# Strided attention and two expert layers on one core: both batches' attention ahead of most of the first layer, and one exponential per slot with its sum

## The chip, the cores and the metric

The kernel runs on one core of one Trainium2 chip. The metric is the time of one execution in microseconds on the device. TensorE (PE in the profile) does matmuls, VectorE (DVE) and ScalarE (ACT) work on tiles in PSUM and SBUF, SyncE (SP) issues DMAs.

## The reference

Attention with 2 batches, 8 heads, 576 positions and head size 64. Heads 0 to 3 see the 32 last positions, heads 4 to 7 see the positions with the same remainder by 32:

```
scores = q @ k.T / sqrt(64)
mask   = (0 <= i - j < 32)               for heads 0 to 3
         (i >= j and i % 32 == j % 32)   for heads 4 to 7
attn   = exp(scores - rowmax), divided by (its row sum + 1e-9)
x      = (attn @ v), as 1152 tokens x 512
h      = ((x @ w1) * (x @ w2)) @ w3 @ w_out          # moe_w1 ... moe_w_out
p      = probs / (row sum + 1e-9)
out    = sum over 4 experts of p[:, e] * (relu(h @ e_w1[e]) @ e_w2[e])
```

The inputs w1, w2, w3 and w_out arrive as 64-bit floats, all others as 32-bit floats.

## The kernel before

**Precision.** A product of two fp32 matrices is done in three matmuls (mm3, lines 245 to 249): each operand is split into a high part (a ScalarE copy that rounds) and a low part (a VectorE subtract), and high x high, low x high and high x low are added up in PSUM.

**Weights.** A 64-bit weight chunk of 128 x 1024 is loaded as pairs of integers and turned to fp32 by a row of steps: round_up (ACT, L136), magnitude (ACT, L144; for the first chunk DVE, L142), clamp, shift, sign, add (DVE, L147 to L157), split_hi (ACT, L164) and split_lo (DVE, L174). There are 20 such chunks: 8 of w12 (both w1 and w2 for 128 columns), 4 of w_out, 8 of w3. A generator, work(), emits their steps in this order, four stops a chunk; advance(n) lets it go n stops on. It is called between other work, so its instructions are woven into the engines' queues, which run in order. add() also issues the load of the chunk two places on (load_next); the raw tiles have two buffers. The variable live counts how many of the 16 buffers for split weights and attention values are in use; while it is over 14, work() doesn't split another chunk. A w12 chunk is freed when its last unit (batch 1, second half) has been emitted.

**Attention.** Each batch has six chunks (Chunk4): three of the local heads (g = 0, six slots of 64 keys per partition) and three of the strided heads (g = 1, eight slots of 54 keys). A chunk goes through scores (PE: a mask matmul and 32 or 48 small ones into one bank of ps_sc), maxima (DVE: row maxima per slot, then scores minus maxima into an SBUF frame), exps (ACT: one Exp over all slots), sums (DVE: sum per slot, + 1e-9, reciprocal), normalise (DVE), transposes (PE) and evac (ACT), pv (PE, two banks), put (ACT, x_hi) and put_lo (DVE, x_lo). The function attend(b, s) is one step of a pipeline of four chunks: scores, maxima and exps of chunk s, sums and normalise of chunk s - 1, transposes and evac of s - 2, pv, put and put_lo of s - 3. Nine steps finish a batch.

**First layer.** A unit (ab_block) is one batch, one of eight column blocks ft and one half of the batch's tokens: 12 matmuls of 288 columns with w1, 12 with w2, a copy (ACT, L444), a product (DVE, L446) and the split of the product (L448, L450). run_unit emits one, with two calls of advance in it. There are 32 units; all of a batch's x is read by each.

**Order of emission.** The queues' order is written out by hand (tc.manual_schedule):

```
for s in range(9):            # batch 0's attention
    attend(0, s)
    keep_warm(12)             # 12 filler matmuls that nobody reads
    if s > 3:
        advance(2)
load_qk(1, 1); load_v_str(1)
while done < 16:              # batch 0's 16 units, batch 1's attention between them
    run_unit()
    if done in (2, 4, 5, 7, 8, 10, 11, 13, 14):
        attend(1, next(steps))
load_probs()
while done < 32:              # batch 1's 16 units
    run_unit()
```

Behind it stand the product of w3 and w_out (wc_tile, eight tiles, wc_acc), the layer x3 with it, and the four experts in 32 steps. PSUM banks: five (pool ps) in turn for transposes, pv results, unit results and filler, three (ps_sc) for scores.

Of the kernel before, what the change touches and what calls it, by code (L numbers as in the profile page):

```python
# [8 lines left out]
F32 = mybir.dt.float32  # L9
# [4 lines left out]
AF = mybir.ActivationFunctionType  # L14
ALU = mybir.AluOpType

B, H, S, D = 2, 8, 576, 64
NT, DM, DFF, E = 1152, 512, 1024, 4
P = 128
# [13 lines left out]
SCALE = 1.0 / float(D) ** 0.5  # L33
# [9 lines left out]
def kernel(  # L43
# [13 lines left out]
    nc = tc.nc  # L57
# [8 lines left out]
    small = ctx.enter_context(tc.tile_pool(name="small", bufs=4))  # L66
# [125 lines left out]
    def load_next():  # L192
        nonlocal loaded
        if loaded < len(stream):
            stream[loaded].raw_load()
            loaded += 1
# [40 lines left out]
    def advance(n=1):  # L237

        return all([next(worker, False) for _ in range(n)])

    def need(c, part=0):
        while not (c.done if part == 0 else c.done1 if part == 1 else c.done2):
            assert advance()
# [12 lines left out]
    def load_qk(b, g, cut=0):  # L256

        tq, tk = (big[b].tile([P, 2, S], F32, tag="big", name=name) for name in ("tq", "tk"))
        pairs = slice(2 * g, 2 * g + 2)
        for c in ([slice(0, cut), slice(cut, S)] if cut else [slice(0, S)]):  # L260
            for t, src, queue in ((tk, kT, nc.sync), (tq, qT, nc.scalar if cut else nc.sync)):
                queue.dma_start(out=t[:, :, c], in_=src[b, pairs, :, c].rearrange("k p n -> p k n"))
        qk[b, g] = (tq, tk)

    def load_v_loc(b, c):

        tv = wp.tile([P, 2, 3, P], F32, tag="w", name="tv_loc")

        def load(dst, rows, t0, n):
            nc.sync.dma_start(out=dst, in_=v_loc[b, :, rows, t0:t0 + n].rearrange("k p t d -> p k t d"))  # L270

        lower, upper, middle = slice(0, 64), slice(64, P), slice(W, 3 * W)
        if c == 0:
            load(tv[lower, :, 0:1], lower, 0, 1)
            load(tv[upper, :, 0:1], middle, 0, 1)
            load(tv[:, :, 1:], slice(0, P), 1, 2)
        elif c == 1:
            load(tv, slice(0, P), 3, 3)
        else:
            load(tv[lower, :, 0:1], lower, 0, 1)  # L280
            load(tv[upper], middle, 3, 3)
            load(tv[lower, :, 1:], middle, 1, 2)
        vals[b, 0, c] = tv

    def load_v_str(b):

        threes = [wp.tile([P, n, P], F32, tag="w", name="tv_str") for n in (8, 4)]
        for tv, t0, n in ((threes[0], 0, 4), (threes[1], 4, 1)):
            for k in range(2):
                nc.sync.dma_start(out=tv[64 * k:64 * k + T3, :2 * n].rearrange("p (h t) d -> p h t d", h=2),  # L290
                                in_=v_str[b, k, :2 * T3, t0:t0 + n].rearrange("(h p) t d -> p h t d", h=2))
        for k in range(2):
            nc.sync.dma_start(out=threes[1][64 * k:64 * k + NB, 2:], in_=v_str[b, k, 2 * T3:2 * T3 + NB, :2])
        vals[b, 1] = threes

    class Chunk4:
# [44 lines left out]

        def maxima(self):
            s = self.slots
            mx = small.tile([P, 8], F32, tag="mx", name="mx")
            nc.vector.tensor_reduce(out=mx[:, :s], in_=self.sc, axis=mybir.AxisListType.X, op=ALU.max)
            self.frame = p_ring[self.index % 4]
            self.p = self.frame[:, :s, :self.nk]
            nc.vector.tensor_tensor(out=self.p, in0=self.sc, in1=self.wide(mx), op=ALU.subtract)

        def wide(self, t):  # L350
            return t[:, :self.slots].unsqueeze(2).to_broadcast([P, self.slots, self.nk])

        def exps(self):
            nc.scalar.activation(self.p, self.p, AF.Exp, scale=SCALE)

        def sums(self):
            s = self.slots
            self.rec = small.tile([P, 8], F32, tag="rec", name="rec")
            rec = self.rec[:, :s]
            nc.vector.tensor_reduce(out=rec, in_=self.p, axis=mybir.AxisListType.X, op=ALU.add)  # L360
            nc.vector.tensor_scalar_add(rec, rec, 1e-9)
            nc.vector.reciprocal(rec, rec)

# [68 lines left out]
    def ab_block(b, ft, n):  # L432
        t = slice(b * S + n * HB, b * S + n * HB + HB)
        if n == 0 and ft % 2 == 0:
            ab_hi[b, ft // 2] = big[b].tile([P, 2, S], F32R, tag="big", name="ab_hi")
            ab_lo[b, ft // 2] = big[b].tile([P, 2, S], F32R, tag="big", name="ab_lo")
        hi, lo = (x[b, ft // 2][:, ft % 2, n * HB:n * HB + HB] for x in (ab_hi, ab_lo))
        ab = tmp.tile([P, HB], F32, tag="pT", name="ab")
        for w in range(2):
            acc = bank("ab_acc")[:, :HB]  # L440
            for k in range(4):
                mm3(acc, c_w12[ft].parts((w * 4 + k) * P, P), (x_hi[:, k, t], x_lo[:, k, t]), k == 0, k == 3)
            if w == 0:
                nc.scalar.copy(ab, acc)  # L444
            else:
                nc.vector.tensor_tensor(out=ab, in0=acc, in1=ab, op=ALU.mult)  # L446
            yield
        nc.scalar.copy(hi, ab)  # L448
        yield
        nc.vector.tensor_tensor(out=lo, in0=ab, in1=hi.bitcast(F32), op=ALU.subtract)  # L450
        yield
# [68 lines left out]
    class Weights:  # L520
# [17 lines left out]
        def work(self):  # L538
# [20 lines left out]
            if self.again:  # L559
                for i, u in enumerate(sums):  # L560
                    nc.sync.dma_start(out=u.bitcast(F32), in_=stored[self.at][i])
            else:
                yield from self.split(sums, w)
                for i, u in enumerate(sums):
                    nc.sync.dma_start(out=stored[self.at][i], in_=u.bitcast(F32))
# [110 lines left out]
    def load_probs():  # L676
        den = const.tile([P, NTT], F32, name="den")
        nc.sync.dma_start(out=pn, in_=probs)
        nc.vector.tensor_reduce(out=den, in_=pn, axis=mybir.AxisListType.X, op=ALU.add)
        nc.vector.tensor_scalar_add(den, den, 1e-9)  # L680
        nc.vector.reciprocal(den, den)
        nc.vector.tensor_tensor(out=pn, in0=pn, in1=den.unsqueeze(2).to_broadcast([P, NTT, E]), op=ALU.mult)
# [4 lines left out]
    with tc.manual_schedule():  # L687
# [3 lines left out]
        p_ring = []  # L691
# [5 lines left out]
        strided_masks()  # L697
        load_v_loc(0, 0)
        load_qk(0, 1)
        load_next()  # L700
        load_v_loc(0, 1)
        load_v_loc(0, 2)
        load_v_str(0)
        load_next()
        load_qk(1, 0)
        for c in range(3):
            load_v_loc(1, c)
        chunks = [[Chunk4(3 * g + c, b, g, c) for g in range(2) for c in range(3)] for b in range(B)]
        units = [(b, ft, i) for b in range(B) for ft in range(8) for i in range(2)]
        done = 0  # L710

        rest = iter(())
# [1 line left out]
        def run_unit():  # L714

            nonlocal done, rest
            b, ft, i = units[done]
            need(c_w12[ft])
            block = ab_block(b, ft, i)
            for _ in range(2):  # L720
                next(rest, None)
                next(block)
                advance(1)
            rest = block
            done += 1
            if b == i == 1:
                c_w12[ft].free()

        def attend(b, s):

            nonlocal live
            chunk = chunks[b]
            n = len(chunk)
            if s < n:
                chunk[s].scores()
                chunk[s].maxima()
                chunk[s].exps()
            if 1 <= s <= n:
                chunk[s - 1].sums()
                chunk[s - 1].normalise()  # L740
            if 2 <= s < n + 2:
                chunk[s - 2].transposes()
                chunk[s - 2].evac(nc.scalar.copy)
            if 3 <= s:
                c = chunk[s - 3]
                c.pv()
                c.put()
                c.put_lo()
                if c.g == 0 or c.c > 0:
                    live -= 1  # L750

        for s in range(9):
            attend(0, s)
            keep_warm(12)
            if s > 3:
                advance(2)
        load_qk(1, 1)
        load_v_str(1)
        steps = iter(range(9))
        while done < 16:  # L760
            run_unit()
            if done in (2, 4, 5, 7, 8, 10, 11, 13, 14):
                attend(1, next(steps))
        load_probs()
        while done < 32:
            run_unit()
        for _ in rest:
            pass
# [4 lines left out]
        for it in range(8):  # L773
# [8 lines left out]
            i = {1: 0, 3: 1, 6: 2}.get(it)  # L782
# [32 lines left out]
        for c in wc[:3]:  # L815
# [6 lines left out]
        steps = [Step(half, e, c, c_e[16 * i + 4 * e + c])  # L822
                 for i, half in enumerate(halves) for e in range(E) for c in range(4)]
# [100 lines left out]
```

## Time and profile before

| | us |
|---|---|
| median of 2 runs | 645.09 (644.95 to 645.22) |
| profiled execution | 647.48 |
| its span, first to last instruction | 645.70 |
| PE busy in the span | 625.6 |
| VectorE busy | 455.9 |
| ScalarE busy | 265.2 |
| mean granted clock of TensorE | 0.992 |

All times in rows are microseconds from the start of the span, durations of single instructions in nanoseconds where a column says mean ns. An idle time in brackets is that of the engine in front of the row, with the instruction that ended it. The matmuls are pipelined, so that a matmul's duration is longer than the distance to the next one's start.

### The profile page before, as it was taken

The page shows a single profiled execution, that of the slowest core. Times are in us where ns is not written, and L with a number is a line of the kernel's source. Part 1 is how long each engine was busy: PE and PEld are TensorE (multiplying, and loading weights), DVE is VectorE, ACT ScalarE, POOL GpSimd, SP SyncE. Part 2 cuts the span into 40 slices and gives each one's busy share as a digit, 9 for nine tenths or more (in the row PEclk, how much of TensorE's full clock was granted, in tenths as well). Part 3 has the DMA queues.
Part 4 walks back from the last instruction along what each step waited for, and adds up shares of the span by engine and source line. Part 5 has one row for each costly group of instructions (what it writes and reads, how often), then busy time and mean ns, then how long its engine had stood idle before and what let it go on. Part 6 is the DMA issues. An engine that isn't in the chain of part 4 may idle for free.

```text
span 645.7 us, 11487 instructions
## 1 busy us (share of the span) xinstructions
PE 625.6 (97%) x4712; PEld 570.3 (88%) x4712; DVE 455.9 (71%) x834; ACT 265.2 (41%) x464; POOL 4.3 (1%) x19
## 2 busy tenths in 40 slices
PE   8788898999999999999999999999999999999997
PEld 6578787999988999998899889998798989999996
DVE  5787998499875423777787787797876576665843
ACT  2546465467655322433333343334433333333321
POOL 2000000000000000000000000000000000000000
PEclk9889999999999999999999999999999999999999
DMA  9846131233543310233444344433478464656321
GB/s 291 245 159 214 66 132 67 67 130 131 171 155 132 125 49 24 66 131 148 177 151 176 131 191 163 168 131 143 183 242 331 162 246 153 222 184 239 131 65 66
DMA packets 28728, 99.45 MB, mean 154 GB/s; under 512 B 2652, under 2 KB 6740, under 8 KB 26116
## 3 DMA queue, kind: packets, MB, share of 16 engines
q1 hardware_dynamic: 28132, 98.14, 43.0%
q8 instruction: 37, 0.61, 0.4%
q10 hardware_dynamic: 544, 0.59, 0.3%
q14 instruction: 15, 0.12, 0.1%
HBM read 79.58 MB, written 19.14 MB: 153 GB/s over the span
## 4 chain that ended last, share of the span: by engine, by line
PE 84%; DVE 8%; DMA 3%; issue 2%; ACT 1%; DVEq 0%; SPq 0%; ACTq 0%
PE g_acc L247 10%; PE g_acc L248 10%; PE g_acc L249 10%; PE m_a L247 4%; PE m_a L249 4%; PE m_a L248 4%; PE ab_acc L249 4%; PE ab_acc L247 4%; PE ab_acc L248 3%; DMA raw<-in_w_dram 3%; PE x_acc L249 3%; PE x_acc L248 3%; PE x_acc L247 3%; PE m_b L248 3%; PE m_c L247 3%; PE m_b L249 3%
## 5 line engine op out<-in xcount | busy, mean ns | idle before, releaser
L596 ACT ACTIVATE h_hi<-u 128x320 fp32r<-128x320 f32 (+1 forms) x128 | 56.9, 445 | 188.5 <-DVE u L602 188.5
L247 PE MATMUL g_acc<-w_hi,h_hi 128*128 128x512 f32 (+1 forms) x296 | 114.3, 386 | 0.0
L248 PE MATMUL g_acc<-w_lo,h_hi 128*128 128x512 f32 (+1 forms) x296 | 114.2, 386 | 0.0
L249 PE MATMUL g_acc<-w_hi,h_lo 128*128 128x512 f32 (+1 forms) x296 | 113.7, 384 | 0.0
L247 PE MATMUL ab_acc<-x_hi,w_hi 128*128 128x288 f32 x256 | 78.0, 305 | 3.4 <-ACT w_hi L164 1.6
L602 DVE TENSOR_TENSOR u<-m_b,u 128x320 f32<-128x320 f32 (+1 forms) x96 | 40.7, 452 | 53.4 <-PE m_b L249 53.4
L535 DVE TENSOR_TENSOR w_lo<-raw,w_hi 128x768 fp32r<-128x768 f32 x64 | 69.4, 1084 | 12.0 <-ACT w_hi L533 12.0
L249 PE MATMUL ab_acc<-x_hi,w_lo 128*128 128x288 f32 x256 | 76.9, 300 | 0.9 <-DVE w_lo L174 0.9
L248 PE MATMUL ab_acc<-x_lo,w_hi 128*128 128x288 f32 x256 | 76.7, 299 | 0.1
L249 PEld LDWEIGHTS g_acc<-w_hi,h_lo 128*128 128x128 f32 x296 | 55.6, 188 | 11.6
L247 PEld LDWEIGHTS g_acc<-w_hi,h_hi 128*128 128x128 f32 x296 | 55.8, 188 | 8.0
L248 PEld LDWEIGHTS g_acc<-w_lo,h_hi 128*128 128x128 f32 x296 | 55.7, 188 | 7.6
L598 DVE SCALAR_TENSOR_TENSOR h_lo<-u,h_hi 128x320 fp32r<-128x320 f32 (+1 forms) x128 | 57.5, 450 | 3.5 <-ACT h_hi L596 1.7
L533 ACT CAST w_hi<-raw 128x768 fp32r<-128x768 f32 x64 | 59.9, 936 | 0.0
L247 PEld LDWEIGHTS ab_acc<-x_hi,w_hi 128*128 128x128 f32 x256 | 49.2, 192 | 4.6 <-ACT x_hi L423 1.8
L249 PEld LDWEIGHTS ab_acc<-x_hi,w_lo 128*128 128x128 f32 x256 | 49.2, 192 | 1.4 <-DVE w_lo L174 1.4
L248 PEld LDWEIGHTS ab_acc<-x_lo,w_hi 128*128 128x128 f32 x256 | 49.3, 193 | 0.3 <-DVE x_lo L427 0.3
L136 ACT ACTIVATE raw<-raw 128x1024 int32<-128x1024 uint32 x20 | 23.2, 1162 | 37.4 <-DMA raw<-in_w3T_dram 20.0
L248 PE MATMUL m_b<-b_t,s_hi 128*128 128x320 f32 (+1 forms) x128 | 37.9, 296 | 0.0
L602 DVE TENSOR_TENSOR u<-m_a,u 128x320 f32<-128x320 f32 (+1 forms) x64 | 28.8, 451 | 11.4 <-PE m_a L249 11.4
L535 DVE TENSOR_TENSOR s_lo<-raw,s_hi 128x1024 fp32r<-128x1024 f32 x16 | 19.6, 1225 | 23.2 <-ACT s_hi L533 23.2
L602 DVE TENSOR_TENSOR u<-m_c,u 128x320 f32<-128x320 f32 (+1 forms) x64 | 28.9, 452 | 4.5 <-PE m_c L249 3.8
(148 smaller groups left out, 1395.1 us busy)
## 6 DMA issues: line engine op xcount, KB each, us to landing
raw<-in_e_dram SPq DMA_DIRECT2D x32, 1024.0 KB
raw<-in_w_dram SPq DMA_DIRECT2D x8, 1024.0 KB
raw<-in_w3T_dram SPq DMA_DIRECT2D x8, 1024.0 KB
stored<-s_hi SPq DMA_DIRECT2D x16, 512.0 KB
stored<-s_lo SPq DMA_DIRECT2D x16, 512.0 KB
s_hi<-stored SPq DMA_DIRECT2D x16, 512.0 KB
s_lo<-stored SPq DMA_DIRECT2D x16, 512.0 KB
raw<-in_w_out_dram SPq DMA_DIRECT2D x4, 1024.0 KB
```

Source lines behind the costliest of these rows:

```text
L136: nc.scalar.activation(self.low, self.low.bitcast(U32), AF.Copy, scale=2.0 ** -29)
L247: mm(acc, lh, rh, start=first, stop=False)
L248: mm(acc, lh, rl, start=False, stop=False)
L249: mm(acc, ll, rh, start=False, stop=last)
L533: nc.scalar.copy(dst[0], src)
L535: nc.vector.tensor_tensor(out=dst[1], in0=src, in1=dst[0].bitcast(F32), op=ALU.subtract)
L596: nc.scalar.activation(hi, src, AF.Relu)
L598: nc.vector.scalar_tensor_tensor(out=lo, in0=src, scalar=0.0, in1=hi.bitcast(F32), op0=ALU.max, op1=ALU.subtract)
L602: nc.vector.tensor_tensor(out=out, in0=acc, in1=b, op=ALU.add)
```

## The change

- The strided chunks' maxima come out negated, are multiplied by the scale into a tile neg, and nothing is subtracted. exps runs eight activations, one per slot of 54 keys, that read the scores in PSUM, with neg as bias, the scale, and the slot's sum as a second output. sums has no reduction left for these chunks. The local chunks stay as they were.
- attend becomes a generator that stops between put and put_lo; filler, worker and unit are emitted between them, so that put_lo stands behind them in VectorE's queue.
- Batch 1's nine attention steps follow batch 0's, with one unit in every second step (units 0 to 3: batch 0, ft 0 and 1) and one stop of the worker in each of the others. Then come batch 1's units of ft 0 and 1, and ft 2 to 7 for both batches.
- The first raw weight load is issued behind the loads of batch 0's second and third local value chunk.

```
         def maxima(self):
             s = self.slots
+            self.frame = p_ring[self.index % 4]
+            self.p = self.frame[:, :s, :self.nk]
+            if self.g == 1:
+                self.neg = small.tile([P, 8], F32, tag="mx", name="neg")
+                nc.vector.tensor_reduce(out=self.neg[:, :s], in_=self.sc, axis=mybir.AxisListType.X, op=ALU.max,
+                                        negate=True)
+                nc.vector.tensor_scalar_mul(self.neg[:, :s], self.neg[:, :s], SCALE)
+                return
...
         def exps(self):
+            self.rec = small.tile([P, 8], F32, tag="rec", name="rec")
+            if self.g == 1:
+                for s in range(self.slots):
+                    nc.scalar.activation(self.p[:, s], self.sc[:, s], AF.Exp, bias=self.neg[:, s:s + 1], scale=SCALE,
+                                         accum_out=self.rec[:, s:s + 1])
+                return
             nc.scalar.activation(self.p, self.p, AF.Exp, scale=SCALE)
 
         def sums(self):
...
+            rec = self.rec[:, :self.slots]
+            if self.g == 0:
+                nc.vector.tensor_reduce(out=rec, in_=self.p, axis=mybir.AxisListType.X, op=ALU.add)
...
         load_qk(0, 1)
-        load_next()
         load_v_loc(0, 1)
         load_v_loc(0, 2)
+        load_next()
         load_v_str(0)
...
-        units = [(b, ft, i) for b in range(B) for ft in range(8) for i in range(2)]
+
+        units = [(b, ft, i) for b in range(B) for ft in range(2) for i in range(2)]
+        units += [(b, ft, i) for ft in range(2, 8) for b in range(B) for i in range(2)]
...
                 c.pv()
                 c.put()
+                yield
                 c.put_lo()
...
         for s in range(9):
-            attend(0, s)
+            step = attend(0, s)
+            next(step, None)
             keep_warm(12)
             if s > 3:
                 advance(2)
+            next(step, None)
         load_qk(1, 1)
         load_v_str(1)
-        steps = iter(range(9))
-        while done < 16:
-            run_unit()
-            if done in (2, 4, 5, 7, 8, 10, 11, 13, 14):
-                attend(1, next(steps))
+        for s in range(9):
+            step = attend(1, s)
+            next(step, None)
+            if s % 2:
+                run_unit()
+            else:
+                advance(1)
+            next(step, None)
         load_probs()
-        while done < 32:
+        while done < len(units):
             run_unit()
```

## Rows read from the trace of the kernel before

**Rows 1.** Windows by stage: busy us by engine (instructions), granted clock, DMA share, GB/s.

```profile
0.00:37.00 37.00, 30.50 (x618) 23.48 (x619) 23.68 (x55) 14.62 (x30) 4.26 (x19) 0.95 0.78 243
37.00:120.00 83.00, 74.23 (x921) 68.86 (x918) 69.89 (x128) 44.68 (x87) 0.00 (x0) 0.96 0.38 128
120.00:180.00 60.00, 60.00 (x420) 58.14 (x420) 51.24 (x77) 35.53 (x56) 0.00 (x0) 1.00 0.38 131
```

**Rows 2.** Timeline of PE, three of its rows with idle time in front.

```profile
20.89 0.67 PE L387 MATMUL o<-pT,tv_loc 64*64 64x32 f32 x33 [2.18 <-issue]
...
41.09 0.40 PE L247 MATMUL ab_acc<-x_hi,w_hi 128*128 128x288 f32 x1 [1.60 <-ACT x_hi L423]
...
109.29 0.40 PE L247 MATMUL ab_acc<-x_hi,w_hi 128*128 128x288 f32 x1 [1.61 <-ACT w_hi L164]
```

**Rows 3.** Timeline: unit 16's product on DVE, the first wc matmul on PE.

```profile
118.52 0.46 DVE L446 TENSOR_TENSOR ab<-ab_acc,ab 128x288 f32<-128x288 f32 x1 [1.24 <-PE ab_acc L249]
...
169.13 0.39 PE L247 MATMUL wc_acc<-w_hi 128*128 128x512 f32 x1
```

**Rows 4.** Groups by line, DVE, 0 to 120 us: busy us, mean ns, idle before.

```profile
L157 DVE CUSTOM_DVE_ANT_0 t<-raw,t 128x2048 uint16<-128x2048 uint16 x9 | 11.0, 1219 | 0.1
L153 DVE SCALAR_TENSOR_TENSOR t<-raw,t 128x1024 int32<-128x1024 int32 x9 | 11.0, 1218 | 0.1
L174 DVE TENSOR_TENSOR w_lo<-t,w_hi 128x1024 fp32r<-128x1024 f32 x8 | 9.7, 1216 | 0.5 <-ACT w_hi L164 0.5
L427 DVE TENSOR_TENSOR x_lo<-o,x_hi 128x192 fp32r<-128x192 f32 (+3 forms) x32 | 9.7, 359 | 5.2 <-ACT x_hi L423 5.2
L446 DVE TENSOR_TENSOR ab<-ab_acc,ab 128x288 f32<-128x288 f32 x16 | 7.2, 452 | 4.5 <-PE ab_acc L249 4.5
L365 DVE TENSOR_TENSOR p_pair<-p_pair,rec 128x384 f32<-128x384 f32 (+1 forms) x12 | 7.0, 584 | 0.4
L348 DVE TENSOR_TENSOR p_pair<-sc,mx 128x384 f32<-128x384 f32 (+1 forms) x12 | 7.0, 583 | 0.6
L345 DVE TENSOR_REDUCE mx<-sc 128x6 f32<-128x384 f32 (+1 forms) x12 | 6.9, 578 | 8.8 <-PE sc L328 6.1 <-PE sc L339 2.8
L360 DVE TENSOR_REDUCE rec<-p_pair 128x6 f32<-128x384 f32 (+1 forms) x12 | 6.8, 568 | 0.0
L450 DVE TENSOR_TENSOR ab_lo<-ab,ab_hi 128x288 fp32r<-128x288 f32 x15 | 6.8, 453 | 2.5 <-ACT ab_hi L448 2.5
L147 DVE TENSOR_SCALAR t<-t 128x1024 f32<-128x1024 f32 x9 | 6.2, 686 | 1.1 <-ACT t L144 1.0
L150 DVE TENSOR_SCALAR t<-t 128x1024 int32<-128x1024 int32 x9 | 6.2, 685 | 0.0
L362 DVE RECIPROCAL rec<-rec 128x6 f32<-128x6 f32 (+1 forms) x12 | 2.4, 197 | 0.4
L361 DVE TENSOR_SCALAR rec<-rec 128x6 f32<-128x6 f32 (+1 forms) x12 | 2.1, 171 | 0.4
```

**Rows 5.** Groups by line and form, ACT, 0 to 120 us.

```profile
L354 ACT ACTIVATE p_pair<-p_pair 128x432 f32<-128x432 f32 x6 | 3.4, 562 | 12.4 <-DVE p_pair L348 12.4
...
L423 ACT CAST x_hi<-o 128x108 fp32r<-128x108 f32 x12 | 3.1, 384 | 1.9 <-PE o L396 1.9
...
L423 ACT CAST x_hi<-o 128x36 fp32r<-128x36 f32 x4 | 1.0, 256 | 0.0
```

**Rows 6.** Timeline of DVE, the end of batch 0's attention.

```profile
41.07 0.87 DVE L427 TENSOR_TENSOR x_lo<-o,x_hi 128x108 fp32r<-128x108 f32 x4 [0.56 <-ACT x_hi L423]
...
42.98 0.69 DVE L147 TENSOR_SCALAR t<-t 128x1024 f32<-128x1024 f32 x1
```

**Rows 7.** Windows of 2 us behind PE's waits at 109.29 and 110.77 us.

```profile
112.00:114.00 2.00, 2.00 (x12) 2.00 (x10) 0.94 (x2) 0.37 (x2) 0.00 (x0) 0.60 0.00 0
114.00:116.00 2.00, 2.00 (x18) 2.00 (x17) 0.68 (x2) 2.00 (x4) 0.00 (x0) 1.00 0.00 0
```

**Rows 8.** Window of 20 us in which DVE is busiest.

```profile
80.00:100.00 20.00, 19.32 (x274) 17.78 (x273) 19.59 (x41) 14.62 (x31) 0.00 (x0) 1.00 0.31 107
```

More of the change, by code (lines that the diff above doesn't have):

```diff
@@ L343, in maxima @@
             s = self.slots
+            self.frame = p_ring[self.index % 4]
[6 more added lines that the diff above has]
+                return
             mx = small.tile([P, 8], F32, tag="mx", name="mx")
             nc.vector.tensor_reduce(out=mx[:, :s], in_=self.sc, axis=mybir.AxisListType.X, op=ALU.max)
-            self.frame = p_ring[self.index % 4]
-            self.p = self.frame[:, :s, :self.nk]
             nc.vector.tensor_tensor(out=self.p, in0=self.sc, in1=self.wide(mx), op=ALU.subtract)
@@ L353, in exps @@
         def exps(self):
+            self.rec = small.tile([P, 8], F32, tag="rec", name="rec")
[4 more added lines that the diff above has]
+                return
             nc.scalar.activation(self.p, self.p, AF.Exp, scale=SCALE)
         def sums(self):
[L357 to L360, printed above, removed]
+            rec = self.rec[:, :self.slots]
+            if self.g == 0:
+                nc.vector.tensor_reduce(out=rec, in_=self.p, axis=mybir.AxisListType.X, op=ALU.add)
             nc.vector.tensor_scalar_add(rec, rec, 1e-9)
```

## The prediction

> **What bounds the kernel now.** I read the windows by stage first [rows 1]. From 120 us on, the PE column equals the length of the window and the granted clock is 1.00: TensorE is the bound and has no gap. Before that it is not: from 37 to 120 us PE is busy 74.23 of 83 us at 0.96, with VectorE at 69.89 of 83, and the first 37 us hold filler matmuls. Later work is the same in both kernels, so the end moves by as much as the point moves at which the 32 units of the first expert layer are done. That point is in [rows 3]: unit 16's product comes at 118.52 us and the first wc_acc matmul at 169.13 us, so a unit costs (169.13 - 118.52) / 16 = 3.16 us where PE is full. Then the gaps of PE in the timeline [rows 2]: 2.18 us in front of a pv matmul (its row names no engine, and the values come by DMA: a transfer), 1.60 us for x_hi, 1.61 us for a w_hi; with three more rows of this kind and two under half a microsecond the idle after 37 us is 8.4 us. The stretch from unit 1 (41.09) to unit 16 (118.52) is 77.4 us; its 16 units need 50.6 and batch 1's attention on PE, by starts of consecutive rows some 2.45 us a chunk, 14.7 (an estimate): 12.1 us are lost there. To gain, the change has to lose less than that.
>
> **The change, part by part.** *Order.* Batch 1's nine attention steps now follow batch 0's with four units among them instead of fourteen or so; 28 units come after them. The sum is: start of the loop + length of the loop + 28 units, against 169.1 us.
>
> *Start.* DVE now ends batch 0 with the last x_lo at 41.07, an add at 41.85 and a clamp at 42.98 of 0.69 us: 43.6 us [rows 6]. In the new kernel a strided chunk loses on DVE the subtract (0.583) and the sum (0.568) and gets a small multiply, for which the 0.171 of L361 stands: 0.98 us less, 2.9 us for three chunks [rows 4]. DVE's rows from 25.56 to 35.1 us follow each other without a gap, so I count all of it: 43.6 - 2.9 = 40.7 us. It is not more, although the raw weight load steps behind two value loads and the wait of 2.18 us goes: ScalarE has the rounding of that same raw chunk in its queue right behind the put, and the first raw then lands about when the value chunk that it let pass landed before, near 22 us (both orders move the same bytes up to there); what PE gains, ACT waits. What is late next there is ACT. The ends are 38.5 (the wait comes out too) and 43.6 us (no gain). Moving x_lo behind the worker's instructions costs nothing in batch 0, where only the next steps' o banks wait for it.
>
> *Eight exponentials for one.* They replace one of 0.562 us [rows 5]. The trace has no activation with a sum output. For 54 elements the nearest forms are casts of 36 (0.256) and 108 elements (0.384): the middle, 0.32, gives 2.56 us a chunk. Below: 0.256 each, 2.05 us. Above: a read-out of the sum as an instruction of its own, at most another 0.256 each, 4.6 us. I take 2.56, since nothing in the trace shows the read-out. That is 2.0 us more on ACT per strided chunk, 6 us a batch. Behind them in ACT's queue stand the evacuation of the chunk before, the put and the worker's round, and PE's pv and DVE's x_lo wait for those; sums and normalise come a step later and have the room. ACT's sum in the loop (9.2 of exponentials, 7.7 of evacuations and puts, 13 of weights and units) is 30 us, below DVE's, so it isn't the bound, but it opens holes in DVE.
> The Trainium skill (ScalarE: Activation LUTs, What ACT_TABLE_LOAD costs) gives an activation with a per-partition bias as 280 + 0.833 N ns with 93 ns of overlap back to back. By that estimate a chunk is 8 x 0.232 + 0.09 = 1.95 us, and the loop some 1 us shorter; no row here shows a pointer bias, and the page has no price for the sum's read-out.
>
> *Length of the loop.* DVE's work in it [rows 4]: six chunks of 0.578 + 0.583 + 0.568 + 0.171 + 0.197 + 0.584 = 2.68 us, 16.1, less 2.9 for the strided ones; 16 x_lo of 0.359, 5.7; from the worker's 13 advances 4 w_lo, 4 shifts, 3 signs, 3 adds and 3 clamps: 4.9 + 2.7 + 3.7 + 3.7 + 2.1 = 17.0; of the four units 4 products and 3 ab_lo: 3.2. Together 39.1 us. PE's work is 4 x 3.16 + 14.7 = 27.4 us, so PE has at least 11.7 us with nothing to do, and no filler stands here. How tightly DVE packs sets the rest: 0.84 in the comparable stretch from 37 to 120 us [rows 1], 0.98 at its best, from 80 to 100 us [rows 8]. I take 0.84: in the new loop DVE meets more waits, not fewer, because the product of a unit stands in its queue ahead of the held-back x_lo, and the unit starts late, behind a transposition that waits for DVE. 39.1 / 0.84 = 46.5 us (39.9 at 0.98). The loop ends at 87.2 us.
>
> *Clock.* After such gaps PE runs slow: between 112 and 114 us, after the two waits near 109 us, the granted clock is 0.60 with 12 matmuls in 2 us, and 1.00 with 18 right behind [rows 7]; that is half and full clock (1.2 and 2.4 GHz). In the loop this is behind DVE. The first unit behind the loop pays for it once: 13 matmuls at 0.24 us start to start instead of 0.13, as in the rows that follow 41.09 us, are 1.4 us; I take 1, with ends of 0 and 1.7.
> The Trainium skill (TensorE: Matmul & The Clock Gate, Part 1) says that throttled is the default state and that activity releases it; it speaks against a loop without filler. By it all four units in the loop would run at half clock, at about twice 3.16 us, 12.6 us more of PE work, which the idle 11.7 would nearly hide.
>
> *The other 28 units.* At full PE 28 x 3.16 = 88.6 us. Their weights are early: a chunk serves four units (12.6 us), and by the order of the worker's steps five are ready at the end of the loop. The earlier release of w12 chunks lets the worker run ahead, which is worth nothing, since from 120 us on PE waits for no weight now [rows 1]. The two moves of raw loads and the probabilities' load past the loop cost nothing: their cover is the same full PE stretch (without it, the row of 1.61 us is the price of a late chunk).
>
> *Sum.* 87.2 + 88.6 + 1 = 176.8 us against 169.1: +7.7. The profiled execution took 647.48 us with a span of 645.70; the median of the runs is 645.09, 2.4 lower. The difference belongs on the median: 652.8, say 652.5.
>
> **The rivals.**
> *DVE packs.* If DVE works at 0.98 as between 80 and 100 us, the loop ends at 40.7 + 39.9 = 80.6, and the sum is 170.2: +1.1, 646. For it: DVE has plenty to do and five PSUM banks loosen the order. Against: in [rows 8] PE had units to fill in, here the steps depend on each other.
> *Batch 0 gains more.* The removed wait comes out in full (start 38.5) and DVE packs: 78.4 + 88.6 = 167.0, -2.1, 643. It needs ACT not to wait for the raw chunk.
> *ACT becomes the bound.* Each slot's sum is read out by an instruction of its own, so a slot is 0.32 + 0.256 = 0.58 us and a strided chunk 4.6 us. Evacuations and puts then come 2.05 us later in three steps of either batch, six in all: +12.3 on +7.7, 665. It decides for slower by 2% (12.9 us) from 5.2 / 48 = 0.11 us over my slot, 0.43 us. Against: such a queue has slack from DVE's surplus in the loop.
> *DVE bounds the units after the loop.* Before the release of chunks stops the worker, it makes a chunk per two units: 5.02 + 2 x 0.905 = 6.8 us of DVE per 6.3 us of PE [rows 4]. Over 16 units that is 4 us, 656.5. Against: five banks carry it, and PE was full between 120 and 180 us with DVE at 51.24 of 60.
>
> **How the numbers follow.** My forecast 0.45 (its own range 648 to 658), packing 0.22, more from batch 0 0.11, ACT 0.13, DVE after the loop 0.09. About 2% is what a measurement of this kernel can tell from no change: below 632.2 faster, above 658.0 slower. No case reaches faster, 0.01 is left for it; slower is ACT's 0.13 and a little of the last, 0.14; within 0.85. The range leaves out ACT's case and some of the fastest: 642 to 660.
>
> **What would show it.** The first wc_acc matmul near 176.8 us is the sum; the first x_hi of batch 1's last chunk near 85 and the last x_lo near 87 us the loop; the end of batch 0's x_lo near 41 us the start; the mean of the new exponentials near 0.32 us the slot; PE busy for about 60% of the loop at a clock below 0.9, DVE near 84%. I am wrong if DVE is much below 80% in the loop with ACT near full (then the slots), if PE has gaps behind the loop, or if batch 0 ends before 39 us.

## The result and the profile after

The changed kernel takes 653.08 us (median of 2 runs, 652.72 to 653.43) against 645.09 us: a ratio of 1.0113 with a 95% interval of 1.0065 to 1.0162. That is slower by about one per cent, clear of no change and inside 2%. The forecast was 652.5 us. Its profiled execution took 652.72 us with a span of 650.9.

The windows of the changed kernel, cut at the ends of its stages (columns as in [rows 1]):

```profile
0.00:39.00 39.00, 33.23 (x735) 26.48 (x736) 26.53 (x61) 23.37 (x82) 4.24 (x19) 1.00 0.84 253
39.00:84.70 45.70, 32.80 (x506) 28.63 (x507) 35.02 (x75) 26.72 (x90) 0.00 (x0) 0.81 0.37 130
84.70:120.00 35.30, 35.30 (x256) 35.30 (x256) 30.71 (x49) 22.65 (x35) 0.00 (x0) 0.95 0.38 127
120.00:174.00 54.00, 54.00 (x410) 54.00 (x409) 41.76 (x64) 30.84 (x53) 0.00 (x0) 1.00 0.36 128
```

Batch 1's attention is a stage of its own now, 39.0 to 84.7 us. In it PE is busy 32.80 of 45.7 us at a mean granted clock of 0.81, DVE 35.02, ACT 26.72. Behind it PE is busy all the time; what is lost there is the slow start of the first unit, at a granted clock of 0.68 from 84.7 to 90.0 us and 1.00 from then on.

The ends of the stages, in the timeline of the changed kernel (they answer to [rows 6] and [rows 3]; columns as there):

```profile
38.32 0.85 DVE L438 TENSOR_TENSOR x_lo<-o,x_hi 128x108 fp32r<-128x108 f32 x4
...
83.99 0.83 DVE L438 TENSOR_TENSOR x_lo<-o,x_hi 128x108 fp32r<-128x108 f32 x4
...
174.25 0.39 PE L247 MATMUL wc_acc<-w_hi 128*128 128x512 f32 x1
```

The last x_lo of batch 0 now starts at 38.32, that of batch 1 at 83.99, and the first wc matmul at 174.25 us instead of 169.13: +5.1, which is the spans' difference (650.9 - 645.7 = 5.2). All of it is there before the first wc matmul. Behind that matmul the two profiles take the same time (645.70 - 169.13 = 476.6 us, 650.9 - 174.25 = 476.6), and so do all profiles of the runs below but one (476.4 to 476.7; 478.0 for the weight load alone).

Who waited for whom between 39 and 85 us in the changed kernel (waiting line, releaser: us in total, times, longest):

```profile
PE tp L381 <- DVE p_pair L376: 8.2, 4, 3.2
ACT p_pair L366 <- DVE p_pair L354: 6.2, 3, 2.3
DVE ab L457 <- PE ab_acc L249: 5.6, 2, 3.7
```

PE waits for DVE's normalise in front of a transposition, and DVE waits for PE's unit in front of a product: the two take turns, with only four units and no filler between the steps.

The exponentials, in the timeline of ACT and as groups by form:

```profile
15.24 0.29 ACT L363 ACTIVATE p_pair<-sc,neg 128x54 f32<-128x54 f32 x1
15.43 0.20 ACT L363 ACTIVATION_READ_ACCUMULATOR p_pair<-sc,neg 128x1 f32 x1
15.52 0.30 ACT L363 ACTIVATE p_pair<-sc,neg 128x54 f32<-128x54 f32 x1
```

```profile
L363 ACT ACTIVATE p_pair<-sc,neg 128x54 f32<-128x54 f32 x48 | 13.9, 315 | 7.9 <-DVE rec L372 4.6 <-DVE neg L350 3.0 <-PE o L398 0.2
...
L363 ACT ACTIVATION_READ_ACCUMULATOR p_pair<-sc,neg 128x1 f32 x48 | 10.3, 216 | 0.0
```

Each sum is read out by an instruction of its own, but these overlap with the exponentials: from one exponential to the next it is 0.28 us (15.24 to 15.52), 2.26 us for eight.

### The profile page after: what moved, and what is told of

The parts are those of the page before. It is cut to its first block, busy times and chain, and to the rows that moved or that the text cites. A ratio compares the mean times of both kernels' runs of the same rounds, so it can differ in the third digit from the quotient of the medians.

```text
span 650.9 us, 11551 instructions
## 1 busy us (share of the span) xinstructions
PE 627.1 (96%) x4712; PEld 573.4 (88%) x4712; DVE 450.3 (69%) x828; ACT 276.7 (43%) x554; POOL 4.2 (1%) x19
## 4 chain that ended last, share of the span: by engine, by line
PE 88%; DVE 6%; ACT 4%; DMA 1%; issue 1%; DVEq 0%; SPq 0%; ACTq 0%
PE g_acc L247 10%; PE g_acc L248 10%; PE g_acc L249 10%; PE ab_acc L247 5%; PE ab_acc L248 5%; PE ab_acc L249 5%; PE m_a L247 4%; PE m_a L249 4%; PE m_a L248 4%; PE x_acc L249 3%; PE x_acc L247 3%; PE x_acc L248 3%; PE m_b L248 3%; PE m_c L247 3%; PE m_b L247 3%; PE m_c L248 3%
```

## Experiments

The theory was that the time is lost in the loop of batch 1's attention, in which VectorE's work, the weight worker's included, has no full TensorE over it. The rivals were the exponentials on ScalarE, the slow clock of TensorE, and the place of x_lo. Each run was set against runs of the kernel before on the same chip, and not all runs were on one chip. The medians of the kernel before are 645.62 us for the exponentials alone, the weight load alone, the change without the exponentials and the held worker; 645.00 for the exponentials with the older steps first, the lean worker, the filler and x_lo in front; 645.78 for the queue's order in the changed kernel and for both edits together; 645.13 for the last run. Between runs of different groups the ratios are to be compared, not the medians.

**One part alone: the exponentials.** The kernel before with the new maxima, exps and sums, as in the change's diff, and nothing else.

> The kernel before with the strided chunks' eight exponentials alone; order, weight loads and x_lo as before. Loop theory (the time of the change is lost in batch 1's attention without units to fill it, the exponentials pay for themselves): VectorE loses 2.9 us of work per batch in a stretch where it is the fullest engine, so 641 to 645 us, likeliest 643. Rival, ScalarE theory (the added ScalarE time is what costs): 2.26 us instead of 0.56 per strided chunk, 10 us in six chunks, so 648 to 655 us.

651.01 us, ratio 1.0087 (1.0060 to 1.0114). My theory missed; in the old order the exponentials cost 5.4 us although they take work from VectorE. The waits of DVE between 37 and 120 us in this kernel:

```profile
DVE x_lo L438 <- ACT x_hi L434: 8.5, 6, 2.3
DVE ab L457 <- PE ab_acc L249: 3.4, 2, 2.6
```

x_lo waits 8.5 us for x_hi, the put that stands behind the eight exponentials in ScalarE's queue. The same line in the kernel before:

```profile
DVE x_lo L427 <- ACT x_hi L423: 4.0, 5, 1.4
```

Batch 0 shows it too. DVE's last clamp there starts at 42.32 us, against 42.98 [rows 6]: 0.66 us earlier, where DVE has 2.9 us less work.

```profile
42.32 0.71 DVE L147 TENSOR_SCALAR t<-t 128x1024 f32<-128x1024 f32 x1
```

**Is it the sum or the queue?** The same kernel, with the older chunks' steps ahead of the exponentials:

```
             if s < n:
                 chunk[s].scores()
                 chunk[s].maxima()
-                chunk[s].exps()
-            if 1 <= s <= n:
-                ...                       # sums, normalise of s - 1
             if 2 <= s < n + 2:
                 ...                       # transposes, evac of s - 2
             if 3 <= s:
                 c.pv()
                 c.put()
+            if s < n:
+                chunk[s].exps()
+            if 1 <= s <= n:
+                ...                       # sums, normalise of s - 1
+            if 3 <= s:
                 c.put_lo()
```

> The kernel before with the eight exponentials (651.0 us) and one more edit: in a step the evacuation, pv and the put of the older chunks are emitted ahead of the exponentials. Queue theory (the exponentials cost because the evacuation and the put stand behind them on ScalarE): 645 to 648 us. Rival, ScalarE's sum (1.7 us a chunk more on ScalarE, wherever it stands): 650 to 652 us.

645.29 us, ratio 1.0003 (0.9980 to 1.0027). The loss is gone with the same exponentials on ScalarE. The same wait, same window:

```profile
DVE x_lo L438 <- ACT x_hi L434: 2.0, 3, 0.8
```

So in the old order it was the queue that cost, not ScalarE's sum. What this reordering does to the kernel before with its one exponential was not run; since x_lo waits less here than in that kernel (2.0 against 4.0 us), a part of what it wins back may have nothing to do with the new exponentials.

**One part alone: the weight load.** The kernel before with load_next() behind load_v_loc(0, 2).

> The kernel before with the first raw weight load moved behind the two value loads, nothing else. Loop theory with a gain in batch 0: the wait of 2.18 us on a value chunk goes, and batch 0 ends 1 to 2 us earlier, 643 to 644.5 us. Rival, as in the prediction's step on the start: ScalarE waits for the raw chunk in its place, 645 us, no change.

645.07 us, ratio 0.9996 (0.9971 to 1.0022): no difference that can be measured. In its one profile the last x_lo of batch 0 starts at 37.87 us, against 41.07 [rows 6], and the first wc matmul at 165.06:

```profile
37.87 0.86 DVE L427 TENSOR_TENSOR x_lo<-o,x_hi 128x108 fp32r<-128x108 f32 x4 [0.43 <-ACT x_hi L423]
...
165.06 0.39 PE L247 MATMUL wc_acc<-w_hi 128*128 128x512 f32 x1
```

One profile against one does not show a gain, though. Of the 4.1 us at the wc matmul this execution loses 1.5 behind it, 0.83 of them in one wait for a w_lo at 199.30 us. And the profiled execution of the kernel before was a late one by 1.9 us against the median of its 23 later runs (643.99 to 648.51; nine of them are above its 647.48). Its wait of 2.18 us for a value chunk [rows 2], which this edit was to remove, is not a matter of the load's place alone: the two kernels above load in the old order as well, and there the same matmuls run in one piece. In the kernel before, with the exponentials alone, and with the older steps first:

```profile
18.28 0.43 PE L387 MATMUL o<-pT,tv_loc 64*64 64x32 f32 x15
18.27 0.90 PE L398 MATMUL o<-pT,tv_loc 64*64 64x32 f32 x48
18.09 0.90 PE L398 MATMUL o<-pT,tv_loc 64*64 64x32 f32 x48
```

So a good part of the 3.2 us at the end of batch 0 may be that execution's own wait. What makes the runs differ was not tried.

**The change without the exponentials.** The changed kernel with the old maxima, exps and sums.

> The changed kernel with the one exponential per strided chunk, its subtract and its sum back; new order, loads and late x_lo stay. Loop theory: VectorE has 2.9 us more per batch and packs as before, so the time is not below the changed kernel's: 653 to 659 us, likeliest 656. ScalarE theory: the loss goes away, 643 to 648 us.

653.20 us, ratio 1.0123 (1.0099 to 1.0147), about the changed kernel's 1.0113. It is at the lower end of what the loop theory gave and far from the ScalarE theory: the new order, with the moved load and the late x_lo, makes all of the loss without the exponentials, and in that order the exponentials neither help nor hurt by anything that can be measured.

**The worker held in the loop.** The changed kernel without the worker's steps in batch 1's attention:

```
-        def run_unit():
+        def run_unit(n=1):
...
-                advance(1)
+                advance(n)
...
             if s % 2:
-                run_unit()
-            else:
-                advance(1)
+                run_unit(0)
```

> The changed kernel with the weight worker held while batch 1's attention runs (no advance in those nine steps, except what a unit needs at once); it goes on with the 28 units behind. Loop theory: some 14 us of VectorE work leave the loop and find cover under full TensorE, so the loop shrinks from 45.7 us to 31 to 37 us: 638 to 645 us, likeliest 641. Rival (the loop's length is latency and a slow TensorE clock, not VectorE's work): the loop stays above 42 us, 649 to 653 us. A second rival: the weights come too late behind the loop and the gain is given back there, 648 us or more with gaps of TensorE behind 80 us.

646.28 us, ratio 1.0000 (0.9975 to 1.0025). Some 7 us of the changed kernel's loss go, no weight is late behind the loop, and the time is a little over the upper end of what I gave. The windows of the loop in this kernel:

```profile
39.80:77.30 37.50, 30.94 (x507) 27.47 (x506) 21.30 (x60) 18.10 (x81) 0.00 (x0) 0.86 0.20 74
```

VectorE has 21.30 us of busy time there instead of 35.02, 13.7 less, and the loop 8.2 less: VectorE was not the whole length. Two waits of PE in this loop were new ones, 2.09 us for batch 1's strided q behind a raw weight in SP's queue and 2.23 us for a w_lo that the held worker hadn't made:

```profile
46.27 1.01 PE L339 MATMUL sc<-tk,tq 64*54 64x54 f32 x32 [2.09 <-DMA tq<-in_qT_dram]
...
63.55 0.40 PE L249 MATMUL ab_acc<-x_hi,w_lo 128*128 128x288 f32 x1 [2.23 <-DVE w_lo L174]
```

**The worker cut to what is needed, q and k early.** From the changed kernel:

```
             keep_warm(12)
-            if s > 3:
-                advance(2)
+            advance((0, 0, 0, 0, 2, 2, 2, 1, 0)[s])
...
             load_v_loc(1, c)
+        load_qk(1, 1)
...
-        load_qk(1, 1)
         load_v_str(1)
...
             if s % 2:
-                run_unit()
-            else:
-                advance(1)
+                run_unit(0)
+            if s < 4:
+                advance(1)
```

> The changed kernel with the worker cut to what units 0 to 3 need: seven stops in batch 0's attention instead of ten, four in batch 1's instead of thirteen; and batch 1's strided q and k are loaded with the first loads, so that they don't stand behind a raw weight. Loop theory: VectorE's work in the loop falls from 39 to about 27 us, the loop takes 30 to 35 us, 636 to 642 us, likeliest 639. Rival (latency of the chain of steps sets the loop, as the held worker's 37.5 us with waits on a transfer and a late w_lo suggests): 644 to 647 us. Second rival: the worker, 9 stops further behind, is late for the wc tiles, gaps there.

642.52 us, ratio 0.9967 (0.9944 to 0.9990): faster than the kernel before by a third of a per cent, just clear of no change, and by less than I expected. The loop:

```profile
36.20:73.20 37.00, 31.82 (x611) 28.13 (x611) 24.02 (x63) 21.03 (x84) 0.00 (x0) 0.91 0.16 52
```

It starts earlier and both waits are gone, but it is still 37 us long, over the 30 to 35 that I gave, with VectorE at 24.02 (0.65) and ScalarE at 21.03 (0.57). Neither is full, which fits the first rival, the latency of the chain of steps, for what is left; it is argued from these shares and not shown. The second rival is out: from the loop to the wc tiles PE waits for no weight, only once, 0.85 us, for ScalarE's copy of a unit's result.

**Filler in the loop.** The changed kernel with keep_warm(12) in the five steps without a unit.

> The changed kernel with 12 filler matmuls in each of the five steps of batch 1's attention that have no unit. Loop theory: filler costs 1.4 us of idle TensorE per step and VectorE stays the pace; only the slow matmuls of units go away, 649 to 653 us, likeliest 651. Clock theory (the half clock in the loop, 0.81 on average, sets its length): 644 to 648 us. If the filler lies in the way of the chain, 655 us or more.

650.58 us, ratio 1.0071 (1.0038 to 1.0105). The interval overlaps that of the changed kernel; in the profile the clock in the loop rises from 0.81 to 0.89 and the loop becomes 0.9 us shorter:

```profile
39.50:84.30 44.80, 36.99 (x562) 32.11 (x562) 34.95 (x74) 26.83 (x90) 0.00 (x0) 0.89 0.37 133
```

So the clock is not the main part of the loop's length, though at 0.89 it is not taken out altogether. The rest of the gain lies behind the loop, where the first unit now runs at 1.00: from the end of the loop to the first wc matmul it is 87.9 us (172.24 - 84.3) instead of 89.6.

**x_lo in front again.** The changed kernel with the yield behind put_lo.

> The changed kernel with x_lo back in front of the filler, the worker and the unit. Loop theory: VectorE's work is the same, so 651 to 655 us. Rival (the x_lo that stands behind a unit's product holds the PSUM banks and so the next step's pv): 645 to 649 us.

654.15 us, ratio 1.0143 (1.0119 to 1.0166). Not faster, so the late x_lo is not the cause of the loss; the microsecond by which the median is higher is inside the intervals. The profiles show that the late x_lo moves time from one stage to another. Here batch 1's first maxima start at 42.92 us, in the changed kernel at 39.06:

```profile
42.92 0.57 DVE L353 TENSOR_REDUCE mx<-sc 128x6 f32<-128x384 f32 x1
39.06 0.56 DVE L353 TENSOR_REDUCE mx<-sc 128x6 f32<-128x384 f32 x1
```

From there to the last x_lo of batch 1 it is 42.3 us here (to 85.24) and 44.9 us in the changed kernel (to 83.99). What DVE's x_lo waits for x_hi up to the end of batch 0, here (0 to 43 us) and in the changed kernel (0 to 39 us):

```profile
DVE x_lo L438 <- ACT x_hi L434: 8.2, 5, 2.3
DVE x_lo L438 <- ACT x_hi L434: 2.9, 3, 1.6
```

**The queue's order in the changed kernel.** The edit of the second run above, in the changed kernel.

> The changed kernel (653.1 us) with the evacuation, pv and put ahead of the exponentials and nothing else. Loop theory: VectorE has 39 us of work in the loop and packs somewhat better, 648 to 652 us, likeliest 650. Queue theory for the whole loss: 645 to 647 us.

651.51 us, ratio 1.0074 (1.0046 to 1.0101): within what the loop theory gave. What was the whole loss in the old order is a small part here at most.

**Both edits together.** The lean worker with that order, and then with x_lo in front as well.

> The lean worker (642.5 us) with the evacuation, pv and put of the older chunks emitted ahead of the exponentials. In its trace VectorE waited 2.2 + 2.2 + 2.8 + 1.7 us in the loop for x_hi and ab_hi that stood behind exponentials. Queue theory: 4 to 7 us of that go, 635 to 639 us, likeliest 637. Rival (the chain exponential, sum, normalise, transposition then comes later and takes the place): 641 to 643 us.

> The kernel of the run above with x_lo in front of filler, worker and unit as well. If a unit's product that VectorE waits for holds x_lo and the banks up, 1 to 2 us less than the run above; if x_lo in front delays normalise and with it the next transposition, 1 to 2 us more.

641.93 us, ratio 0.9913 (0.9882 to 0.9944), and 640.53 us, ratio 0.9898 (0.9868 to 0.9929). Against the kernel before on its own chip the first gains 3.9 us by the medians, and the lean worker 2.5: 1.4 us more, not the 4 to 7 of the queue theory, and the two intervals touch, so even that stays unclear. The second has the lowest time of the study, 1.4 us under the first by the medians as its first case had it, but their intervals overlap. Both are faster than the kernel before by about one per cent, clear of no change. The loop of the second:

```profile
38.10:73.50 35.40, 30.66 (x550) 27.47 (x539) 24.21 (x62) 21.24 (x84) 0.00 (x0) 0.90 0.14 45
```

**The fastest kernel without the exponentials.** The same with the old maxima, exps and sums.

> The fastest kernel so far (lean worker, evacuation, pv, put and x_lo ahead of the filler and units, 640.5 us) with one exponential per strided chunk, the subtract and the sum as before. Where neither VectorE (0.69 of the loop) nor ScalarE (0.59) is full, the form of the exponentials should matter little: 639 to 642 us, and what the lean worker gained is the order's alone. If the 2.9 us of VectorE work per batch count, 643 to 646 us; if the eight exponentials cost on the chain, 636 to 638 us.

642.24 us, ratio 0.9950 (0.9926 to 0.9973). Between the first two cases that I gave: against the kernel before on its own chip it gains 2.9 us by the medians, with the eight exponentials 5.3 us. The two intervals still overlap a little, so a gain by the exponentials is likely here and not shown.

## Why the prediction was right

The forecast time and its sign hold, and the stage is the one that was named: the loop without cover loses more than the order saves. That the total came within 0.6 us is luck, since two errors of about 2.5 us cancel in it. The steps one by one:

- **PE full behind the loop.** Right: 84.70 to 174.00 us without a gap, 174.25 - 84.70 = 89.6 us for 28 units, with 88.6 + 1 forecast. No weight is late, and VectorE does not bound the units.
- **Length of the loop.** 46.5 us forecast, 45.7 measured, but by two errors that cancel. I counted the right instructions (the trace has the 4 w_lo, 4 shifts, 3 signs, 3 adds and 3 clamps of the worker, and the 4 products), and their durations add up to about 39 us there as well. But I divided this sum by a share made of busy time. Neighbouring instructions overlap in the records, so the busy time of the same work is less: 35.02 us. And DVE's share was 35.02 / 45.7 = 0.77, not 0.84. That the worker's instructions in the loop are a large part of its length is shown by the held worker (37.5 us).
- **Start of the loop.** 40.7 us forecast, about 39.1 measured. The size is near, the terms are others. DVE's shorter work was to give 2.9 us; alone it gives 0.66 (the exponentials alone), because x_lo then waits for the puts behind the exponentials, 8.0 us up to 43 us against 3.2 in the kernel before. The late x_lo, which I put at nothing in batch 0, takes most of these waits out: without it the changed kernel's loop starts 3.9 us later. ScalarE did not wait for the raw chunk in place of PE's value wait either: its round starts at 22.44 us without a wait, and VectorE reads the raw chunk at 20.18.

```profile
22.44 1.20 ACT L136 ACTIVATE raw<-raw 128x1024 int32<-128x1024 uint32 x1
...
20.18 0.69 DVE L142 TENSOR_SCALAR t<-raw 128x1024 int32<-128x1024 int32 x1
```

- **The sum against the median.** The profiles differ by 5.2 us, the forecast by steps was 7.7, and the medians differ by 8.0. The profiled execution of the kernel before was 2.4 us over its median. Its 169.13 us hold that, since behind the first wc matmul it is no longer than the others (476.6 us); the wait of 2.18 us for a value chunk is the likeliest part. I carried the whole difference of the steps to the median, where 169.13 should have been lower. The steps were 2.5 us too long, and the base 2.4 us too late; the total came out by both.
- **Exponentials.** 2.56 us a chunk forecast, 2.26 measured. The read-out by an instruction of its own exists, which I took not to be there, and costs little since it overlaps. The Trainium skill (ScalarE: Activation LUTs, What ACT_TABLE_LOAD costs) gives, as an estimate by its formula, 280 + 0.833 x 54 = 325 ns for the exponential, and the trace has 315; the 232 ns from one to the next that follow from its overlap are 280 ns here, where the read-out stands between.
- **Rivals.** ScalarE as the bound: refuted in the new order (the change without the exponentials is as slow), yet in the old order the mechanism that I had put there, the evacuation and the put behind the exponentials, is real: with these emitted first the loss of 5.4 us is gone. Packing at 0.98: refuted by 0.77. Batch 0 gaining more: the start was near that rival's 38.5, but DVE didn't pack; its sum also leaves out the 1 us for the clock that the other sums have.
- **Clock.** The 1 us behind the loop is right in kind: 13 matmuls from 86.11 to 89.22 us start 0.24 us apart instead of 0.13, 1.4 us. In the loop PE is busy 72% of the time at 0.81, where I gave about 60%: 32.80 us against the 27.4 that I counted. Two of its four units run half or more of their matmuls at 0.24 us. The filler run's profile shows what this is worth: 0.9 us of the loop and 1.6 behind it.
- **Where the gain went.** Weights that serve both batches at once ease the worker only behind the loop, and there PE was already full before. What the order gives up is cover: batch 1's nine steps stood among twelve units (the third to the fourteenth) and now stand among four.

What stays open: the loop of 35 to 37 us in the lean kernels, with PE's work of 27.4 us by my count and neither DVE nor ACT full, was put down to latency by the shares only; no run took it apart. What makes runs of one kernel differ is open as well.

## What to carry to other kernels

Before steps with long chains are moved together, count the work that would stand under them; if side work such as a weight worker is woven in, let it emit only what is needed there and leave the rest for the stretch that is full anyway. Long instructions in a queue that runs in order cost what stands behind them, so emit older chunks' evacuations first: here eight short exponentials in front of them cost 5.4 us in the old order, and nothing that can be measured behind them. A queue order that costs nothing in one form of a kernel can cost in another: moving x_lo back ends batch 0 by 0.8 us earlier with one exponential per strided chunk (40.46 to 39.67 us) and by 3.9 with eight (43.02 to 39.17; one profile each). And one profiled execution is one draw: its stages should be laid against the spread of the runs before a difference is added to their median.

## What the runs showed of the hardware

An activation with a sum output appears as two instructions, ACTIVATE (315 ns for 54 elements) and ACTIVATION_READ_ACCUMULATOR (216 ns), and eight such pairs back to back take 2.26 us, 0.28 us a pair. In the changed kernel's profile TensorE, 1.6 us after a wait of 2.40 us and in full work, ran at a granted clock of 0.50 from 86.2 to 89.1 us (the lower of its two levels, 1.2 GHz): matmuls of 288 columns start 0.24 us apart there, before and behind that 0.13. Runs of one kernel differ by more than 1% (643.04 to 651.07 us over 25 runs of the kernel before on one chip).
